# A long convolution by FFT and a gated layer: the exchanged spectrum made by matmuls instead of loaded, and the taps, transposes and first stage in a new order

## The chip, the cores and the metric

The kernel runs on one core of one Trainium2 chip. The metric is device time in microseconds; a lower number is better. A core has a matrix engine (TensorE, PE; its weight loads are listed as PEld), a vector engine (VectorE, DVE), a scalar engine (ScalarE, ACT), GpSimd (POOL) and SyncE (SP), which here only issues DMAs. The engines run side by side, each in its own order of instructions, and wait for each other by semaphores.

## What is computed

All data are float32; the sequence has 2048 rows of 448 channels.

```
mod = (silu(c) @ w_mod)                      # six rows: sa, ca, ga, sb, cb, gb
h   = layernorm(x) * (1 + ca) + sa           # x = A_q
k'  = sum over 4 taps of shift_k[:, t] * k shifted by t rows
kv  = k' * v
y   = irfft(rfft(kv padded to 4096) * rfft(ssm_k padded to 4096))[:2048] + kv * ssm_D
x   = x + ga * h * y
h   = layernorm(x) * (1 + cb) + sb
x   = x + gb * ((sigmoid(h @ w_gate) * (h @ w_up)) @ w_down)
```

## The kernel before

The long convolution is done as a transform in two stages of matmuls. Both the filter (ssm_k, tiles ak[0] and ak[1], one for each half h of the 448 channels) and the product kv (tiles av[0], av[1]) pass through it. Stage 1 (lines 199 and 208) multiplies by a table zc; then `turn` (line 176) transposes 32x32 squares on DVE, 128x896 at a time, eight such pieces to a tile; stage 2 (`stage2`, line 267) multiplies by the table w2, in eight blocks n = 0 to 7 to a half. A block of a spectrum has 128 rows: two groups of 64, and in each 32 rows of real and 32 of imaginary parts.

The order of the work is written out by hand; the scheduler keeps it, and each engine does its part in that order.

**First part, up to about 81 us.** The filter's stage 1 for both halves, DVE's transposes of ak[0], and stage 2 of the filter for half 0 (`stage2_k(0, n)`; matmuls to a PSUM pair "t", copied back by ACT, line 274). ak[1] isn't transposed by DVE: `turn_out` writes it to DRAM (kd) and `turn_in` reads it back in the other order (lines 183, 188). In between stands the short convolution: four groups i of rows by four channel tiles ct of 112 channels. For ct 0 and 1 ACT makes the first tap's product (line 238) and DVE adds the other three (line 240). For ct 2 and 3 ACT makes the products of taps 0 and 3, POOL those of taps 1 and 2 (lines 233, 235), and the four products are added in PSUM by the transposes. `conv_turn` (line 254) transposes the results on PE into the PSUM tiles kv, which take the tags "sa", "y" and "t" in turns; `conv_mul` (line 260) multiplies v by them on DVE. Then stage 1 of v, one matmul pair for each of 16 groups (`stage1_v`), copied out by ACT and, for half 1 from group 8 on, by DVE (line 212).

**Half 0 and half 1 of the product.** `stage2_v(h, between)` makes stage 2 of v for block n and multiplies it by the filter's spectrum. A complex product needs v times the filter (line 303) and v times the filter with real and imaginary rows exchanged (line 304). The exchanged copy kx is loaded by `load_kx`: four DMAs a block from the filter's tile in SBUF to another one, 32 rows each, one block ahead (line 288). `stage2_back` (lines 314 to 316) does the first stage back for the block before it. Between the blocks, `during0` and `during1` put other work: loads of x, `turn_in`, transposes of av, the six rows of mod (`mod_load` DMAs two halves of 392 KB, `mod_parts` and `mod_sum` multiply them on PE and ACT), the statistics of the first layer norm on ACT (`ln1_stats`, two tiles of x at a time, lines 410 and 411), the gate rows G (`gates`: ACT line 430, POOL lines 431 and 432), and for half 1 `stage2_k(1, n)`.

**After that**, `stage_out` (line 325) makes y, gates multiply it into x (lines 338 and 339, on POOL for half 0 and on DVE for half 1), the second layer norm is taken (lines 391 to 404, xn in line 698), and the gated layer runs on PE to the end (lines 739 and 761).

PSUM holds two pairs of banks with the tag "t", one with "sa" and one with "y"; a tile waits until the last reader of the one before it in its tag is done. All loads of this part are issued by SP, in order: a DMA that must wait for its buffer holds up all those behind it.

Of the kernel before, what the change touches and what calls it, by code (L numbers as in the profile page):

```python
# [17 lines left out]
P = 128  # L18
# [6 lines left out]
def _dft_tables():  # L25
# [13 lines left out]
    w2 = np.zeros((128, 64))  # L39
    for r in (0, 64):  # L40
        w2[r:r + 32, :32] = e.real
        w2[r + 32:r + 64, :32] = -e.imag
        w2[r:r + 32, 32:] = e.imag
        w2[r + 32:r + 64, 32:] = e.real
# [36 lines left out]
def adaln_conv_glu_kernel(ctx: ExitStack, tc: tile.TileContext, q, kT, v, ssm, shift, dskip,  # L81
# [66 lines left out]
    w2 = small([P, 64], "w2")  # L148
# [53 lines left out]
    def stage1_v(g):  # L202
# [6 lines left out]
        for h in range(2):  # L209
            a, y = av[h].rearrange("p (s j) c -> p s j c", s=2)[:, :, g], pt[:, :, h * C:h * C + C]  # L210
            if h and g > 7:
                DVE.tensor_copy(a, y)
            else:
                ACT.activation(a, y, AF.Copy)
# [3 lines left out]
    def conv_taps(i, ct, some=(0, 1, 2, 3)):  # L218


        for tap in some:
            x = ktl[:, ct, 4 * i + 3 - tap:4 * i + 7 - tap]
            w = sk[:, ct, tap:tap + 1]
            if tap == 3:
                a = x
            elif tap == 0 or ct > 1:
                a = pk.tile([DT, 4, P], F32, tag="accp" if ct > 1 else "accs", bufs=8 if ct > 1 else 2, name=f"acc{i}_{ct}{tap}")
            else:
                a = acc[i, ct][0]
            if ct > 1:  # L230
                acc.setdefault((i, ct), []).append(a)
                if tap in (0, 3):
                    ACT.activation(a, x, AF.Copy, scale=w)
                else:
                    POOL.tensor_mul(a, x, w.unsqueeze(2).to_broadcast([DT, 4, P]))  # L235
            elif tap == 0:
                acc[i, ct] = [a]
                ACT.activation(a, x, AF.Copy, scale=w)
            else:
                DVE.scalar_tensor_tensor(a, x, w, acc[i, ct][0], op0=OP.mult, op1=OP.add)  # L240
                acc[i, ct] = [a]
# [3 lines left out]
    def conv_turn(i, cts, es=(0, 1)):  # L245

        for e in es:
            if (i, e) not in kvs:
                kvs[i, e] = two((("sa", "y"), ("t", "t"), ("sa", "y"), ("t", "sa"))[i][e], f"kv{i}{e}")
            for ct in cts:  # L250
                parts = acc[i, ct]
                for g in range(2):
                    for k, a in enumerate(parts):
                        PE.matmul(kvs[i, e][:, g, ct * DT:ct * DT + DT], a[:, 2 * e + g], ident[:DT, :DT],
                                  start=k == 0, stop=k == len(parts) - 1, is_transpose=True)
# [6 lines left out]
    def stage2(pt, x):  # L262

        for b in range(2):
            for r in (0, 64):
                c = r ^ 64 * b
                PE.matmul(pt[c:c + 64, b, :D], w2[r:r + 64], x[r:r + 64, b], start=True, stop=True)  # L267

    def stage2_k(h, n):

        x = block(ak[h], n)
        pt = two("t", f"s2k{h}_{n}")
# [8 lines left out]
    kxs = {}  # L281

    def load_kx(h, n):

        kx = quad("kx", 2, f"kx{h}_{n}").rearrange("p a c -> p (a c)").rearrange("p (b j c) -> p b j c", b=2, c=DT)
        x = block(ak[h], n)
        for r in range(0, P, 32):
            nc.sync.dma_start(kx[r:r + 32], x[r ^ 32:(r ^ 32) + 32])  # L288
        kxs[h, n] = kx

    products = []

    def stage2_v(h, between):

        cols4 = lambda t: t.rearrange("p b (j c) -> p b j c", c=DT)
        for n in range(8):
            kx = kxs.pop((h, n))
            if n < 7 or h == 0:
                load_kx(*((h, n + 1) if n < 7 else (1, 0)))
            pt = two("t", f"s2v{h}_{n}")  # L300
            stage2(pt, block(av[h], n))
            m = [pairs(quad("m", 4, f"m{h}_{n}_{k}")) for k in range(2)]
            DVE.tensor_mul(cols4(m[0]), cols4(rows(pt)), block(ak[h], n))  # L303
# [587 lines left out]
```

## Time and profile before

| | |
|---|---|
| runs timed | 657.83 us median of 3 (657.61 to 660.26) |
| profiled execution | 658.9 us, span 657.1 us from first to last instruction |
| mean granted TensorE clock | 0.955 |
| busy, us | PE 583.3, PEld 439.5, DVE 344.0, ACT 254.2, POOL 95.4 |
| DMA | 51.84 MB in 37207 packets, of them 19379 under 512 B |

The page divides the span into slices and gives each engine's busy share; a window of the trace does so for a stretch between two times. The granted clock is the TensorE clock that the throttle let through, 1.00 being full speed. The chain of waits is followed back from the last instruction: each piece is work, a transfer or an issue that what comes next waited for. In a timeline each row has its start in us, its length, the engine, the line of the code, the operation, output and input by name; in brackets stands the idle time before it and what ended that. In a row that ends in "x2" two instructions are merged. f32 matmuls show twice in the records, so eight records of line 267 are the four matmuls of a block.

### The profile page before, as it was taken

To read this page: it belongs to the slowest core of one execution; us is meant where nothing else is said; L and a number is where in the kernel's file an instruction comes from. 1 tells how busy PE (TensorE), PEld (TensorE's weight loads), DVE (VectorE), ACT (ScalarE), POOL (GpSimd) and SP (SyncE) were. 2 spreads that over 40 slices of the span, in tenths; PEclk is the share of its full clock that TensorE was granted. 3 is DMA by queue.
4 is the path that set the end of the run, shared out by engine and by line. 5 is a ranking of instruction groups with operands and counts; after the bars stand their busy time and mean duration, and the time that the engine had idled before them with its cause. 6 is when DMAs were issued, how large, how long until landed. Compare 5 with 4: busy or idle time off the path is not lost.

```text
span 657.1 us, 7479 instructions
## 1 busy us (share of the span) xinstructions
PE 583.3 (89%) x2976; PEld 439.5 (67%) x2976; DVE 344.0 (52%) x403; ACT 254.2 (39%) x448; POOL 95.4 (15%) x65
## 2 busy tenths in 40 slices
PE   7867875489854998999999999999999999999995
PEld 6445311123333776888888888888888888888884
DVE  0998496488988875543234443244333433333322
ACT  4874466258742657851122222122112212221110
POOL 1282002200998100000000000010001000000000
PEclk9998977699987997999999999999999999999999
DMA  8994599958610110000001111011101100000122
GB/s 294 237 297 136 167 265 256 219 115 197 170 57 16 60 33 1 0 1 0 1 29 48 31 30 49 0 29 33 32 15 30 33 17 18 11 0 1 57 83 84
DMA packets 37207, 51.84 MB, mean 79 GB/s; under 512 B 19379, under 2 KB 25909, under 8 KB 37045
## 3 DMA queue, kind: packets, MB, share of 16 engines
q1 hardware_dynamic: 37108, 51.36, 29.2%
q8 instruction: 23, 0.38, 0.2%
q14 instruction: 12, 0.09, 0.0%
q0 software_dynamic: 64, 0.01, 0.0%
HBM read 36.68 MB, written 7.34 MB: 67 GB/s over the span
## 4 chain that ended last, share of the span: by engine, by line
PE 62%; DVE 10%; ACT 8%; DMA 5%; issue 2%; SPq 1%; DVEq 0%; ACTq 0%
PE gu L739 37%; PE d L761 19%; DVE av L176 3%; DMA kx<-ak 3%; DMA wb<-in_wmod_dram 2%; PE sa L314 1%; SPq L288 1%; PE s2v L267 1%; DVE xn L698 1%; PE y L325 1%; DVE x L339 1%; PE s2k L267 1%; ACT xn L700 1%; ACT full L720 1%; DVE wt L469 1%
## 5 line engine op out<-in xcount | busy, mean ns | idle before, releaser
L739 PE MATMUL gu<-xt,wt 128*128 128x512 f32 x1232 | 292.4, 391 | 0.6 <-DVE xt L728 0.6
L739 PEld LDWEIGHTS gu<-xt,wt 128*128 128x128 f32 x1232 | 231.0, 188 | 48.6 <-DVE xt L728 1.1
L743 DVE TENSOR_TENSOR sg<-sg,gu 128x512 f32<-128x512 f32 x56 | 38.5, 688 | 190.4 <-ACT sg L742 190.3
L761 PE MATMUL d<-wt,hh 128*128 128x448 f32 x448 | 129.6, 371 | 6.5 <-ACT wt L463 3.2
L742 ACT ACTIVATE sg<-gu 128x512 f32<-128x512 f32 x56 | 33.5, 598 | 240.6 <-PE gu L739 240.5
L761 PEld LDWEIGHTS d<-wt,hh 128*128 128x128 f32 x448 | 84.9, 190 | 17.6 <-ACT wt L463 3.7
L761 PE MATMUL d<-wt,hl 128*128 128x448 f32 x224 | 82.8, 369 | 0.1
L762 DVE TENSOR_TENSOR x<-x,d 128x896 f32<-128x896 f32 x56 | 60.5, 1080 | 6.4 <-PE d L761 6.4
L747 DVE TENSOR_TENSOR hl<-sg,hh 128x512 fp32r<-128x512 f32 x56 | 38.8, 693 | 39.2 <-ACT hh L746 39.2
L462 POOL TENSOR_TENSOR r<-r,gbrow 128x448 f32<-128x448 f32 x10 | 11.5, 1158 | 319.4 <-DMA r<-in_wd_dram 319.4
L176 DVE STREAM_TRANSPOSE av<-av 128x896 f32<-128x896 f32 x32 | 56.9, 1835 | 0.0
L746 ACT ACTIVATE hh<-sg 128x512 fp32r<-128x512 f32 x56 | 35.4, 633 | 47.2 <-DVE sg L743 47.2
L761 PEld LDWEIGHTS d<-wt,hl 128*128 128x128 f32 x224 | 42.7, 190 | 3.8 <-DVE hl L747 0.4
L315 PE MATMUL sa<-m,wa 128*64 128x448 f32 x64 | 31.9, 627 | 5.5 <-DVE m L304 5.5
L314 PE MATMUL sa<-m,wa 128*64 128x448 f32 x64 | 31.4, 613 | 3.6 <-DVE m L303 2.3
L431 POOL TENSOR_TENSOR G<-G,arow 128x896 f32<-128x896 f32 x8 | 18.5, 2308 | 99.5 <-ACT G L430 51.0
L267 PE MATMUL s2k<-ak,w 64*64 64x448 f32 x128 | 17.1, 579 | 13.5 <-DMA kx<-ak 7.8
L235 POOL TENSOR_TENSOR acc<-kT,sk 112x512 f32<-112x512 f32 x16 | 22.1, 1409 | 18.1 <-DMA kT<-in_kT_dram 13.3
L325 PE MATMUL y<-av,wb 128*64 128x224 f32 x128 | 15.4, 398 | 9.7 <-DVE av L176 9.0
L304 DVE TENSOR_TENSOR m<-s2v,kx 128x896 f32<-128x896 f32 x16 | 17.4, 1089 | 12.4 <-DMA kx<-ak 12.4
L314 PEld LDWEIGHTS sa<-m,wa 128*64 128x64 f32 x64 | 7.9, 149 | 23.5 <-issue 12.9
L316 ACT ACTIVATE av<-sa 128x896 f32<-128x896 f32 x16 | 14.6, 911 | 22.5 <-PE sa L315 22.5
(108 smaller groups left out, 568.5 us busy)
## 6 DMA issues: line engine op xcount, KB each, us to landing
kx<-ak SPq DMA_DIRECT2D x64, 112.0 KB, 5.2
kd<-ak SPq DMA_DIRECT2D x4, 896.0 KB, 7.1
x<-in_q_dram SPq DMA_DIRECT2D x4, 896.0 KB, 10.1
ak<-kd SPq DMA_DIRECT2D x4, 896.0 KB, 12.7
out_dram<-x SPq DMA_DIRECT2D x8, 448.0 KB, 2.5
wb<-in_wmod_dram SPq DMA_DIRECT2D x8, 392.0 KB, 7.0
v<-in_v_dram SPq DMA_DIRECT2D x6, 448.0 KB, 12.4
r<-in_wg_dram SPq DMA_DIRECT2D x10, 256.0 KB, 2.7
```

The source lines that it names most:

```text
L176: DVE.transpose(x, x)
L235: POOL.tensor_mul(a, x, w.unsqueeze(2).to_broadcast([DT, 4, P]))
L267: PE.matmul(pt[c:c + 64, b, :D], w2[r:r + 64], x[r:r + 64, b], start=True, stop=True)
L314: PE.matmul(pt[0:64, b, :D], wa[:, b, 0:64], m1[:, b], start=True, stop=True)
L315: PE.matmul(pt[64:128, b, :D], wa[:, b, 64:128], m2[:, b], start=True, stop=True)
L739: PE.matmul(pgu[:, s], w[:, t, f * P:(f + 1) * P], x[:, xs], start=i == 0, stop=i == len(ops) - 1)
L742: ACT.activation(sg, pgu[:, 0], AF.Sigmoid)
L743: DVE.tensor_mul(sg, sg, pgu[:, 1])
L746: ACT.activation(hh, sg, AF.Copy)
L747: DVE.tensor_sub(hl, sg, hh)
L761: PE.matmul(pt[:, i, :D], h[:, (2 * e + i) * P:(2 * e + i + 1) * P], w[:, f], start=m == 0, stop=m == len(ops) - 1)
L762: DVE.tensor_add(x1[:, g:g + 2], x1[:, g:g + 2], rows(pt))
```

## The change

Three things are changed, and the order around them.

1. The table w2 becomes two: the second has the columns of real and imaginary output exchanged. `stage2_v` multiplies every block of v by both and so gets v and its exchanged form, in two PSUM pairs "t" (one for each group of 64 rows' parity b). DVE multiplies each pair by the filter's block, which is repeated over the two forms by a stride of zero. `load_kx` and its 64 DMAs are gone. `stage2_k` for half 1 uses the tag "y" instead of "t".
2. POOL makes no tap products. For ct 2, group 0 uses matmuls by a diagonal matrix of the taps (made once by POOL, in arow), groups 1 to 3 have four ACT products added by the transposes; ct 3 has that in group 0 and ACT and DVE like ct 0 and 1 in the others. So ACT makes 27 products instead of 24 and DVE 33 adds instead of 24.
3. Stage 1 of v starts between the groups of the short convolution, the tiles kv always take "sa" and "y", and ACT copies groups 8 and 9 of half 1, which DVE did. The turn-in of ak[1] and the loads of x move ahead of the halves; the rows of mod, the statistics and the gate rows come at other blocks, and row 4 already in block 1.

```diff
-    w2 = np.zeros((128, 64))
+    w2 = np.zeros((128, 2, 64))
     for r in (0, 64):
...
+        x = np.block([[e.real, e.imag], [-e.imag, e.real]])
+        w2[r:r + 64, 0] = x
+        w2[r:r + 64, 1] = np.roll(x, 32, 1)
...
-            if h and g > 7:
+            if h and g > 9:
                 DVE.tensor_copy(a, y)
...
+    def conv_first(i, ct):
+        acc[i, ct] = [pk.tile([DT, 4, P], F32, tag="accs", bufs=3, name=f"acc{i}_{ct}")]
+        ACT.activation(acc[i, ct][0], ktl[:, ct, 4 * i + 3:4 * i + 7], AF.Copy, scale=sk[:, ct, 0:1])
+    def conv_rest(i, ct):
+        for tap in range(1, 4):
             x = ktl[:, ct, 4 * i + 3 - tap:4 * i + 7 - tap]
+            a = x if tap == 3 else acc[i, ct][0]
+            DVE.scalar_tensor_tensor(a, x, sk[:, ct, tap:tap + 1], acc[i, ct][0], op0=OP.mult, op1=OP.add)
+        acc[i, ct] = [a]
+    def conv_products(i, ct):
+        acc[i, ct] = []
+        for tap in range(4):
+            x = ktl[:, ct, 4 * i + 3 - tap:4 * i + 7 - tap]
+            a = x if tap == 3 else pk.tile([DT, 4, P], F32, tag="accp", bufs=6, name=f"acp{i}_{tap}")
+            ACT.activation(a, x, AF.Copy, scale=sk[:, ct, tap:tap + 1])
+            acc[i, ct].append(a)
...
-                kvs[i, e] = two((("sa", "y"), ("t", "t"), ("sa", "y"), ("t", "sa"))[i][e], f"kv{i}{e}")
+                kvs[i, e] = two(("sa", "y")[e], f"kv{i}{e}")
...
+                    if (i, ct) not in acc:
+                        for tap in range(4):
+                            PE.matmul(y, ktl[:, ct, 4 * i + 3 - tap + 2 * e + g], diag[:, tap], start=tap == 0, stop=tap == 3)
...
     def stage2_k(h, n):
-        pt = two("t", f"s2k{h}_{n}")
+        pt = two("y" if h else "t", f"s2k{h}_{n}")
...
         for n in range(8):
-            kx = kxs.pop((h, n))
-            if n < 7 or h == 0:
-                load_kx(*((h, n + 1) if n < 7 else (1, 0)))
-            pt = two("t", f"s2v{h}_{n}")
-            stage2(pt, block(av[h], n))
-            m = [pairs(quad("m", 4, f"m{h}_{n}_{k}")) for k in range(2)]
-            DVE.tensor_mul(cols4(m[0]), cols4(rows(pt)), block(ak[h], n))
-            DVE.tensor_mul(cols4(m[1]), cols4(rows(pt)), kx)
+            x, k = block(av[h], n), block(ak[h], n)
+            pts = [two("t", f"s2v{h}_{n}_{b}") for b in range(2)]
+            for ex in range(2):
+                for b in range(2):
+                    for r in (0, 64):
+                        c = r ^ 64 * b
+                        PE.matmul(pts[b][c:c + 64, ex, :D], w2[r:r + 64, ex], x[r:r + 64, b], start=True, stop=True)
+            m = [pairs(quad("m", 4, f"m{h}_{n}_{b}")) for b in range(2)]
+            for b in range(2):
+                DVE.tensor_mul(cols4(m[b]), cols4(rows(pts[b])), k[:, b].unsqueeze(1).to_broadcast([P, 2, 4, DT]))
...
     def during0(n):
...
-        if n < 4:
-            turn_in(ak[1], kd, (n,))
...
+        if n > 1:
+            stage2_k(1, n - 2)
+        if n < 2:
+            mod_parts({0: 2, 1: 4}[n], "y")
+            mod_load({0: 3, 1: 5}[n])
+        if n in (1, 2, 6):
+            ln1_end({1: 0, 2: 1, 6: 2}[n])
+        if n in (2, 4, 6):
             next(gating)
+        if n not in (2, 4, 6):
+            ln1_stats({0: 2, 1: 3, 3: 4, 5: 5, 7: 6}[n])
...
-        if 2 <= n < 8:
+        if 1 <= n < 6:
             next(gating)
```

What stands in the engines' orders now: first the loads on SP, from the last turn-out of ak[1] to the loads for block 2 of half 0. wb and wm are halves of the rows of mod (wb also holds two tiles of v), x_670 and x_629 are x. Before:

```order
L183 DMA kd<-ak_150 256x1x896 x2
L351 DMA wb<-in_wmod_dram 112x896 x2
L351 DMA wm_671<-in_wmod_dram 112x896
L351 DMA wm_673<-in_wmod_dram 112x896
L585 DMA x_670<-in_q_dram 128x1792
L595 DMA wa<-in_wat_dram 128x256
L288 DMA kx_0_705<-ak_149 32x8x112 x4
L351 DMA wm_710<-in_wmod_dram 112x896
L351 DMA wm_712<-in_wmod_dram 112x896
L288 DMA kx_1_754<-ak_149 32x8x112 x4
L585 DMA x_670<-in_q_dram 128x1792
L188 DMA ak_150<-kd 32x32x224
```

In the changed kernel, behind the same turn-out and up to row 4 of mod (wm_700, with its second half behind it):

```order
L187 DMA ak_154<-kd 32x32x224 x2
L344 DMA wm_621<-in_wmod_dram 112x896
L344 DMA wm_623<-in_wmod_dram 112x896
L581 DMA x_629<-in_q_dram 128x1792
L590 DMA wa<-in_wat_dram 128x256
L344 DMA wb<-in_wmod_dram 112x896 x2
L344 DMA wm_662<-in_wmod_dram 112x896
L344 DMA wm_664<-in_wmod_dram 112x896
L581 DMA x_629<-in_q_dram 128x1792
L187 DMA ak_154<-kd 32x32x224 x2
L581 DMA x_629<-in_q_dram 128x1792 x2
L344 DMA wm_700<-in_wmod_dram 112x896
```

The read-back of ak[1] and all of x now stand ahead of row 4, and the exchanged copies are gone.

Then PE around block 2 of half 0; s2v is the second stage of v, sa the first stage back, s2k the filter's second stage for half 1, and mod_903 and mod_775 are row 4. Before:

```order
L371 MATMUL mod_772<-part_781,ones 128x448
L267 MATMUL s2v_2_823<-av_484,w_78 64x448 x4
L314 MATMUL sa_1_832<-m_1_0_795,wa 64x448
L315 MATMUL sa_1_832<-m_1_1_796,wa 64x448
L314 MATMUL sa_1_832<-m_1_0_795,wa 64x448
L315 MATMUL sa_1_832<-m_1_1_796,wa 64x448
L267 MATMUL s2v_3_859<-av_484,w_78 64x448 x4
```

In the changed kernel:

```order
L364 MATMUL mod_731<-part_740,ones 128x448
L355 MATMUL mod_775<-wm_700,scb 32x224 x4
L355 MATMUL mod_775<-wm_702,scb 32x224 x4
L293 MATMUL s2v_2_0_795<-av_405,w_78 64x448 x2
L293 MATMUL s2v_2_1_796<-av_405,w_78 64x448 x2
L293 MATMUL s2v_2_0_795<-av_405,w_78 64x448 x2
L293 MATMUL s2v_2_1_796<-av_405,w_78 64x448 x2
L308 MATMUL sa_1_809<-m_1_0_760,wa 64x448 x2
L308 MATMUL sa_1_809<-m_1_1_761,wa 64x448 x2
L374 MATMUL mod_775<-ones,part_784 128x1 x3
L376 MATMUL mod_775<-ones,part_784 64x1 x2
L266 MATMUL s2k_0_823<-ak_154,w_78 64x448 x4
```

Row 4's matmuls now stand ahead of block 2's second stage, where they stood behind block 4; s2v has twice the matmuls, and s2k of the other half follows from block 2 on, not from block 4.

More of the change, by code (lines that the diff above doesn't have):

```diff
@@ L488, in adaln_conv_glu_kernel @@
     POOL.tensor_mul(sc, sc, cv)
+    diag = arow[:DT].rearrange("p (a d) -> p a d", d=DT)
+    for tap in range(4):
+        POOL.tensor_mul(diag[:, tap], ident[:DT, :DT], sk[:, 2, tap:tap + 1].to_broadcast([DT, DT]))
     POOL.tensor_copy(scb, sc.unsqueeze(2).to_broadcast([DT, 4, 32]))
@@ L512, in adaln_conv_glu_kernel @@
         load_v(k)
[L513 to L518 removed]
     kd = pd.tile([P, 32, C], F32, name="kd")
+    for i in range(2):
+        turn_out(ak[1], kd, i)
     av = []
```

209 lines of the change are left out of this document (80 added, 129 removed).

## Prediction

> **What bounds the kernel now.** I read the busy shares over the span first, then the windows of four stages, then the chain of waits, the DMA view, and the timelines of DVE and PE. The change touches nothing behind the run-up to the last stage, so what can move lies in the first 212 us. The stages by window (columns: length, then busy us of PE, PEld, DVE, ACT and POOL, then granted clock, DMA share, GB/s), the two halves of the spectrum product first, then the run-up to the last stage, then the taps and first stage of v:
>
> ```profile
> 88.20:145.50 57.30, 39.38 (x206) 11.10 (x208) 38.46 (x34) 29.96 (x65) 8.34 (x4) 0.76 0.97 211
> 145.50:181.40 35.90, 31.72 (x236) 11.21 (x237) 32.53 (x30) 28.51 (x56) 17.51 (x9) 1.00 0.73 181
> 181.40:211.90 30.50, 14.22 (x104) 9.07 (x100) 28.07 (x27) 11.48 (x21) 29.69 (x14) 0.78 0.10 32
> 24.10:81.20 57.10, 43.80 (x304) 25.11 (x304) 46.54 (x44) 34.84 (x58) 22.10 (x16) 0.94 0.71 205
> ```
>
> Half 0 takes 57 us, half 1 36 us for the same eight blocks. In half 0 no engine is busy over 40 of the 57 us, but the DMA engines are (0.97). The chain of waits says the same:
>
> ```profile
> 91.33 12.24 DMA wb<-in_wmod_dram
> ...
> 105.52 9.12 DMA kx<-ak
> ...
> 122.75 6.04 DMA kx<-ak
> ```
>
> One queue carries all of it. Its loads (count, KB each, us to landing), and its rate from 92 to 128 us:
>
> ```profile
> kx<-ak SPq DMA_DIRECT2D x64, 112.0 KB, 5.2
> kd<-ak SPq DMA_DIRECT2D x4, 896.0 KB, 7.1
> x<-in_q_dram SPq DMA_DIRECT2D x4, 896.0 KB, 10.1
> ak<-kd SPq DMA_DIRECT2D x4, 896.0 KB, 12.7
> wb<-in_wmod_dram SPq DMA_DIRECT2D x8, 392.0 KB, 7.0
> ```
> ```profile
> DMA packets 8937, 8.64 MB, mean 240 GB/s; under 512 B 4279, under 2 KB 8375, under 8 KB 8936
> ```
>
> The landmarks for the sum are on DVE: the last copy of the first stage, the five transposes, the first product of half 0, of half 1, and the last product:
>
> ```profile
> 80.69 0.62 DVE L212 COPY av<-s1v 128x448 f32<-128x448 f32 x1 [0.60 <-ACT av L214]
> 81.23 8.60 DVE L176 STREAM_TRANSPOSE av<-av 128x896 f32<-128x896 f32 x5
> 89.72 1.06 DVE L303 TENSOR_TENSOR m<-s2v,ak 128x896 f32<-128x896 f32 x1
> ...
> 145.56 1.09 DVE L303 TENSOR_TENSOR m<-s2v,ak 128x896 f32<-128x896 f32 x1 [0.86 <-issue]
> ...
> 180.33 1.08 DVE L304 TENSOR_TENSOR m<-s2v,kx 128x896 f32<-128x896 f32 x1
> ```
>
> So before: first stage to 81.3, 8.4 to the first product, half 0 55.9, half 1 35.8 (to 181.4), run-up 30.4 (to 211.8, below), and 445.3 of what I leave alone.
>
> **The taps and the first stage.** One tap add on DVE beside a GpSimd product, and two stretches after GpSimd had stopped:
>
> ```profile
> 42.70 2.97 DVE L240 SCALAR_TENSOR_TENSOR acc<-kT,sk,acc 112x512 f32<-112x512 f32 x2
> ...
> 60.27 0.75 DVE L240 SCALAR_TENSOR_TENSOR kT<-kT,sk,acc 112x512 f32<-112x512 f32 x1
> 60.94 2.08 DVE L260 TENSOR_TENSOR wb<-wb,kv 128x896 f32<-128x896 f32 x2
> 62.93 1.53 DVE L240 SCALAR_TENSOR_TENSOR acc<-kT,sk,acc 112x512 f32<-112x512 f32 x2
> ```
>
> An add costs 1.48 beside GpSimd and 0.77 without it. The change drops the 16 GpSimd products (22.1 us, row of 24.10 above) and makes 33 adds where there were 24. DVE is free of its first transposes at 30.5 as before; from there 33 x 0.77 = 25.4, 8 products x 1.04 = 8.3, and six copies where there were eight, at the pace of 1.17 of the copies before 81.3, 7.0: 71.2. ACT in turn gets 27 tap products for 24 and two more copies (line, engine, shapes, count, busy, mean ns; those of L430, L411 and L410 are used further down):
>
> ```profile
> L430 ACT ACTIVATE G<-x,nmr,rstd 128x224 f32<-128x224 f32 x32 | 15.7, 564 | 1.0 <-DVE nmr L419 1.0
> ...
> L274 ACT ACTIVATE ak<-s2k 128x896 f32<-128x896 f32 x16 | 14.4, 908 | 9.4 <-PE s2k L267 9.4
> ...
> L214 ACT ACTIVATE av<-s1v 128x448 f32<-128x448 f32 x24 | 12.0, 548 | 11.5 <-PE s1v L208 11.5
> ...
> L411 ACT ACTIVATE gbrow<-x,nmr 128x448 f32<-128x448 f32 x16 | 10.7, 670 | 0.5
> ...
> L410 ACT ACTIVATE gbrow<-x 128x448 f32<-128x448 f32 x16 | 9.2, 575 | 0.3
> ...
> L238 ACT ACTIVATE acc<-kT,sk 112x512 f32<-112x512 f32 x8 | 5.8, 721 | 0.7 <-DVE kT L240 0.7
> ```
>
> 27 x 0.72 + 8 x 0.91 + 26 x 0.55 = 41 us from 25 on: 66, less than DVE. The tap results now always go to the same two PSUM pairs, so the transposes of group i+1 wait for the products of group i; I add 1.8 for these hand-overs. The 16 matmuls with the diagonal are not in the trace; the nearest are the transposes they replace in part, which PE has room for until DVE frees the second half of the spectrum at 30.5: nothing. The first stage ends at 73.0, 8.3 earlier; bounds 71.2 and, if the hand-overs eat it all, 81.3 (not later, since both engines have less work in sum than the 57 us there).
>
> **First product.** Five transposes, 8.6, end at 81.6. PE reaches it through two modulation rows, the first of which now stands behind x, wa and another row in the queue; I take 1 us for that and put the first product at 82.5, 9.5 behind the copies (+1.1).
>
> **Half 0.** The 64 kx loads (7.3 MB) go, and with them the waits of the chain. In their place PE makes the exchanged spectrum. One block of PE before:
>
> ```profile
> 135.31 0.98 PE L267 MATMUL s2k<-ak,w 64*64 64x448 f32 x8
> 136.12 0.93 PE L267 MATMUL s2v<-av,w 64*64 64x448 f32 x8
> 136.98 0.59 PE L314 MATMUL sa<-m,wa 128*64 128x448 f32 x1
> ...
> 138.63 0.98 PE L267 MATMUL s2k<-ak,w 64*64 64x448 f32 x8
> ```
>
> From start to start: s2k 0.81, s2v 0.86, sa 1.65. The new s2v is twice that, 1.72, so a block is 4.2 with s2k and 3.4 without. The two products of a block keep size and count; a factor repeated by a zero stride is new, and I price it by the rows of 1.06 and 1.08. Both PSUM pairs "t" now serve one block, so s2v of block n+1 waits for the products of block n; sa, s2k on PE and the transposes on DVE lie in that gap.
>
> Blocks 0 and 1 are DVE's: 2.0 for the products and 3.5 for two transposes each, 82.5 to 93.5, and two row products, 1.3: 94.8. Then PE has modulation row 4 ahead of s2v of block 2, and that row now stands in the queue behind everything: from the last turn-out on, four ak<-kd, four x, eight halves of modulation rows, 10.7 MB with wa. The turn-out waits only for the first four groups of the first stage: 30.5, nine adds and two products (9.0), and for each group ACT's two copies and its share of the tap products, about 2, in all about 48; v and kd are then issued (1.4) and kd lands 7.1 later (its row): 56.5. At 250 GB/s, a little over the 240 of the row since no 448-byte packets are among them, 42.8 us: row 4 lands at 99.3, not by 94.8. Bounds for the landing: 96 (three quarters of the bytes at 300 or more) and 102 (240, one us late). This rate is where the Trainium skill speaks differently. "DMA: Bandwidth & Descriptors", Specifications, gives about 358 GB/s from HBM for a core and line rate from 512 bytes a packet, which these packets of 896 bytes and more all pass; by an estimate from it the 10.7 MB would take 30 us and row 4 would be there by 87, a rival below.
>
> So row 4 (1.0) and most of s2v (1.5) follow 99.3, and block 2's products start at 101.8. Block 3 stands behind ACT, since its s2k waits in the single "y" pair for the row's results: part 0.5, statistics of two tiles 2 x (0.58 + 0.67 + two accumulator reads) = 3.1, the copy of sa 0.9, columns, copy of s2k: 5.8, 107.6. From there each block costs ACT two copies of 0.9 and either statistics (3.1, three blocks) or a gate row (4 x 0.49, two blocks): 4.4; PE 4.2, DVE 2.0 + 1.75. Five blocks at 4.4: 129.6. Half 0 is 47.1 instead of 55.9: -8.8.
>
> **Half 1.** kx no longer limits it, but it was DVE's before (32.5 of 35.9 us) and stays so. Block to block: 4.1 (PE), 5.8, then 5.5 three times (products and two transposes), 3.4 behind s2v (y, 1.7 on PE, in between), 4.9, and 2.0: 36.7, +0.9.
>
> **Run-up.** Lines of DVE before, and what GpSimd was doing:
>
> ```profile
> 181.33 12.12 DVE L176 STREAM_TRANSPOSE av<-av 128x896 f32<-128x896 f32 x7
> ...
> 198.08 2.18 DVE L339 TENSOR_TENSOR x<-x,G 128x896 f32<-128x896 f32 x1
> ...
> 203.23 1.15 DVE L404 SCALAR_TENSOR_TENSOR nmr<-mv,rstd 128x4 f32<-128x4 f32 x1
> 204.31 0.68 DVE L469 TENSOR_TENSOR wt<-tmp,wt 128x512 fp32r<-128x512 f32 x1
> 204.91 6.90 DVE L698 TENSOR_SCALAR xn<-x,rstd,nmr 128x448 f32<-128x448 f32 x4
> ...
> 219.54 1.09 DVE L339 TENSOR_TENSOR x<-x,G 128x896 f32<-128x896 f32 x1
> ```
> ```profile
> 209.05 2.51 POOL L462 TENSOR_TENSOR tmp<-tmp,gbrow 128x448 f32<-128x448 f32 x2
> ```
>
> The same x<-x,G is 2.18 while GpSimd works and 1.09 after it. In the change the statistics come earlier, and with them GpSimd's 24 gate operations of 2.1 (8.34 for four, row of 88.20). The last gate row is ready about 158, ten such operations and the 2.5 above follow: 182. xn would start 23.5 behind the last product as before (204.9 - 181.4), less what x and nmr save, at 188: GpSimd is done some 5 us ahead of it. Then x saves 1.1, nmr 1.0, and xn falls from 6.9 to between 6.9 (no gain) and four of the 0.62 of the copy of equal size, 2.5; I take 2.5 as the nearest: -6.5 in all. "VectorE: DVE Perf Modes", in its perf-mode tier table of the Trainium skill, has such an operation at 1227 ns for 2048 columns, by an estimate 0.3 for 448; by it xn would be 1.1, 1.4 us better still. The other DVE lines and the last stage stay.
>
> **Sum.** -8.3 + 1.1 - 8.8 + 0.9 - 6.5 = -21.6. The profiled execution took 658.9 (span 657.1), 1.1 over the median of the three runs: 658.9 - 21.6 - 1.1 = 636.
>
> **Rivals.**
> Row 4 lands in time: then block 2 starts 4.5 earlier, at the row products' end, and the time is 632; with the other upper ends (first stage at 71.2) 627. For it: half of the packets behind the 240 were the 448-byte ones that go. Against: 211 and 205 over whole stretches, the second with none of them. The skill's figure above would give this case.
>
> The first stage stays as long: hand-overs through one pair of PSUM tiles and an in-order SP queue, where x and all behind it wait for the last tap tile. Then the queue, too, starts 8 us later: 636 + 8.3 = 644, and 651 if GpSimd's end also falls behind xn (6.5). For it: ACT and DVE alternate with PE after every group. Against: DVE was busy 46.5 of 57 us there, 11 of them lost to GpSimd and more in waits.
>
> Slower than before: PE becomes the bound at a low clock. Per block PE, DVE and PE again alternate through the same two pairs; PE has 16 x 3.4 + 8 x 0.8 + about 9 for modulation and y = 70 us at full clock in both halves. The gains outside them are 13.7, so the halves may take 91.7 + 13.7 = 105: below a mean granted clock of 0.67 the kernel is slower; at 0.60 it would be 117 and 669 in all. The row of half 0 shows 0.76 with long DMA waits, that of half 1 1.00 with PE at 88%. With fuller PE I expect the latter. "TensorE: Matmul & The Clock Gate", the part on psum-queue depth-cycling, describes this throttling from short idles between groups; by half 1's row it does not happen here.
>
> **How the numbers follow.** Forecast (630 to 643) 0.47, row 4 in time (624 to 632) 0.25, first stage without gain (643 to 651) 0.18, below 624 0.02, no change 0.05 (nearly every gain lost; within 0.5%, about what a measurement of this kernel can tell), slower 0.03. The range reaches over the first three: 624 to 649. Faster by over 0.5% is 0.92, same 0.05, slower 0.03.
>
> **What would show it.** Right: tap adds at 0.75 throughout; last copy of the first stage at 71 to 75; the wait of the chain near 95 to 100 on modulation row 4, none on kx; blocks 3 to 7 at 4.2 to 4.6; half 1 near 37; xn well under 1 us each, GpSimd done before them. Wrong: a granted clock under 0.7 in the halves, the first product after 88, half 0 over 52, GpSimd still busy beside xn.

## The result, and the profile after

The changed kernel takes 639.18 us (median of 4 runs, 637.25 to 640.29), the kernel before 657.95 beside it: a ratio of 0.9704, 95% interval 0.9672 to 0.9737. Predicted were 636.0 and 624 to 649. The profiled execution took 639.4 (span 637.6, before 657.1).

The stretches by window of the trace (length, busy us of PE, PEld, DVE, ACT and POOL with their instructions, then granted clock, DMA share, GB/s): taps and first stage, the way to the first product, half 0, half 1, run-up.

```profile
24.10:70.00 45.90, 39.48 (x268) 21.64 (x260) 41.65 (x52) 36.39 (x62) 0.00 (x0) 0.96 1.00 291
70.00:86.50 16.50, 10.52 (x56) 2.88 (x60) 8.39 (x5) 6.59 (x17) 0.00 (x0) 0.59 1.07 264
86.50:129.40 42.90, 36.92 (x278) 13.38 (x280) 37.43 (x36) 32.45 (x70) 10.38 (x5) 0.92 0.38 106
129.40:167.60 38.20, 36.16 (x276) 14.10 (x278) 32.32 (x28) 26.19 (x53) 26.75 (x14) 1.00 0.21 75
167.60:192.20 24.60, 14.20 (x103) 9.27 (x99) 23.92 (x26) 9.92 (x17) 16.22 (x9) 0.79 0.12 33
```

The transfers that filled half 0 (share 0.97) now fill the two stretches ahead of it. Half 0 is bound by the engines, and the new weak place is the row of 70.00, where every engine waits and TensorE has a granted clock of 0.59. The landmarks on DVE, the same as those of before: last copy of the first stage, first product, blocks 1 to 3, first product of half 1, last product, and the run-up:

```profile
68.61 1.38 DVE L211 COPY av<-s1v 128x448 f32<-128x448 f32 x2 [0.95 <-ACT av L213]
...
86.53 2.09 DVE L296 TENSOR_TENSOR m<-s2v,ak 128x896 f32<-128x896 f32 x2 [8.14 <-PE s2v L293]
...
91.91 2.10 DVE L296 TENSOR_TENSOR m<-s2v,ak 128x896 f32<-128x896 f32 x2
...
97.66 0.68 DVE L367 TENSOR_TENSOR brow<-brow,mod 128x448 f32<-128x448 f32 x1
...
103.39 2.09 DVE L296 TENSOR_TENSOR m<-s2v,ak 128x896 f32<-128x896 f32 x2 [4.77 <-PE s2v L293]
...
109.12 2.08 DVE L296 TENSOR_TENSOR m<-s2v,ak 128x896 f32<-128x896 f32 x2
...
129.39 2.09 DVE L296 TENSOR_TENSOR m<-s2v,ak 128x896 f32<-128x896 f32 x2 [0.16 <-PE s2v L293]
...
165.53 2.09 DVE L296 TENSOR_TENSOR m<-s2v,ak 128x896 f32<-128x896 f32 x2 [1.15 <-PE s2v L293]
...
179.46 5.14 DVE L462 TENSOR_TENSOR wt<-tmp,wt 128x512 fp32r<-128x512 f32 x3
184.52 1.07 DVE L331 TENSOR_TENSOR G<-G,y 128x896 f32<-128x896 f32 x1
185.63 1.09 DVE L332 TENSOR_TENSOR x<-x,G 128x896 f32<-128x896 f32 x1
...
190.39 1.78 DVE L684 TENSOR_SCALAR xn<-x,rstd,nmr 128x448 f32<-128x448 f32 x4
```

| stretch, us | before | predicted | after |
|---|---|---|---|
| end of the first stage | 81.3 | 73.0 | 70.0 |
| from there to the first product | 8.4 | 9.5 | 16.5 |
| half 0 | 55.9 | 47.1 | 42.9 |
| half 1 | 35.8 | 36.7 | 38.2 |
| run-up, to the end of xn | 30.4 | 23.9 | 24.6 |
| the rest | 445.3 | 445.3 | 445.4 |

The gains stand where they were expected, but three terms missed, by -3.0, 7.0 and -4.2 us, and cancel: that the sum came within 3.2 us of the time is in part luck. The column "before" is one execution. In three experiments below that keep the old taps and run-up (the spectrum alone and the two that follow it) the first stage ended at 76.2 to 78.5 and the run-up took 28.4 to 29.1, so these two gains lie between 6 and 11 us and between 4 and 6. The two waits that are left show on PE:

```profile
74.23 0.97 PE L355 MATMUL mod<-wb,scb 112*32 112x224 f32 x8 [5.49 <-DMA wb<-in_wmod_dram]
75.51 0.97 PE L355 MATMUL mod<-wb,scb 112*32 112x224 f32 x8 [0.31 <-DMA wb<-in_wmod_dram]
77.20 1.86 PE L364 MATMUL mod<-part,ones 128*128 128x448 f32 x2 [0.71 <-ACT part L357]
78.99 1.72 PE L355 MATMUL mod<-wm,scb 112*32 112x224 f32 x16
81.44 1.86 PE L364 MATMUL mod<-part,ones 128*128 128x448 f32 x2 [0.72 <-ACT part L357]
83.23 3.27 PE L293 MATMUL s2v<-av,w 64*64 64x448 f32 x16
...
98.44 1.72 PE L355 MATMUL mod<-wm,scb 112*32 112x224 f32 x16 [5.45 <-DVE rstd L411]
100.09 3.27 PE L293 MATMUL s2v<-av,w 64*64 64x448 f32 x16
```

The first is plain: row 1 of mod lands at 74.2, and its matmuls, its sum, row 0's and its sum all stand ahead of the first s2v. The second needs care. Row 4's matmuls (98.44) need two things: row 4 itself, and the PSUM pair "y", which DVE reads last in L367 (97.66 + 0.68 = 98.34, above). DVE's order puts that behind two transposes. When row 4 was issued, and how long it took to land (two halves):

```profile
L344 SPq DMA_DIRECT2D wm<-in_wmod_dram x2: 338/392/445, 82.0 to 83.0; - x2
...
DMA to landing us min/median/max: 15.3/15.6/15.8
```

So the first half landed at 97.3 to 97.8 and the second, which is needed about 0.9 later, at some 98.6. Load and PSUM pair came free within a microsecond of each other; by these times, removing only one would have gained under 1 us. The bracket names L411, another instruction of DVE right behind L367.

### The profile page after: what moved, and what is told of

It reads as the page before. It is cut to its first block, busy times and chain, and to the rows that moved or that the text cites. A ratio compares the mean times of both kernels' runs of the same rounds, so it can differ in the third digit from the quotient of the medians.

```text
span 637.6 us, 7551 instructions
## 1 busy us (share of the span) xinstructions
PE 589.6 (92%) x3084; PEld 443.8 (70%) x3084; DVE 335.7 (53%) x410; ACT 256.1 (40%) x453; POOL 72.1 (11%) x53
## 4 chain that ended last, share of the span: by engine, by line
PE 59%; DVE 7%; ACT 6%; issue 1%; DVEq 0%; ACTq 0%
PE gu L725 39%; PE d L747 20%; DVE wt L462 2%; ACT xn L686 1%; ACT full L706 1%; DVE sg L729 1%; DVE x L332 1%; DVE x L748 1%; DVE G L331 1%; ACT xt L710 1%; ACT hh L732 1%; ACT sq L385 1%; PE pt L698 1%; DVE xt L712 1%; DVE av L175 1%
## 5 line engine op out<-in xcount | busy, mean ns | idle before, releaser
L296 DVE TENSOR_TENSOR m<-s2v,ak 128x896 f32<-128x896 f32 x32 | 33.2, 1079 | 18.2 <-PE s2v L293 18.0
L293 PE MATMUL s2v<-av,w 64*64 64x448 f32 x256 | 33.6, 596 | 1.8 <-DVE m L296 1.6
L424 POOL TENSOR_TENSOR G<-G,arow 128x896 f32<-128x896 f32 x8 | 16.9, 2108 | 115.4 <-ACT G L423 115.4
L308 PE MATMUL sa<-m,wa 128*64 128x448 f32 x128 | 27.7, 554 | 0.0
L293 PEld LDWEIGHTS s2v<-av,w 64*64 64x64 f32 x256 | 11.8, 143 | 19.1 <-issue 10.9
L308 PEld LDWEIGHTS sa<-m,wa 128*64 128x64 f32 x128 | 7.9, 138 | 18.9 <-issue 9.6
L318 PEld LDWEIGHTS y<-av,wb 128*64 128x64 f32 x128 | 11.3, 161 | 13.8 <-issue 10.5
L462 DVE TENSOR_TENSOR wt<-r,wt 128x512 fp32r<-128x512 f32 (+1 forms) x30 | 19.7, 661 | 0.0
```

The costliest lines, as they stand in the source:

```text
L293: PE.matmul(pts[b][c:c + 64, ex, :D], w2[r:r + 64, ex], x[r:r + 64, b], start=True, stop=True)
L296: DVE.tensor_mul(cols4(m[b]), cols4(rows(pts[b])), k[:, b].unsqueeze(1).to_broadcast([P, 2, 4, DT]))
L308: PE.matmul(pt[r, b, :D], wa[:, b, r], m[b][:, ex], start=True, stop=True)
L462: DVE.tensor_sub(lo, r, hi)
```

## The experiments

The theory is the prediction's: three gains that add up (the taps without GpSimd, half 0 without kx and with its loads ahead, a run-up that GpSimd no longer slows), and two waits. The rivals: one part alone does it; the queue bounds half 0 in any order; TensorE's doubled work is what limits now. In each run the kernel before was timed on the same chip, and the ratios are to it. Two experiments may stand on different chips, where the kernel before took 657.7 to 659.4, so differences between their medians are good to some 1.7 us.

### The exchanged spectrum alone

The kernel before, with the doubled w2, `stage2_v` and the tag of s2k as in the change; row 4's matmuls and the sums of rows 3, 4 and 5 of mod are shifted by a block so that "y" is free for s2k.

```diff
-            kx = kxs.pop((h, n))
...
+            for ex in range(2):
+                for b in range(2):
+                    for r in (0, 64):
+                        c = r ^ 64 * b
+                        PE.matmul(pts[b][c:c + 64, ex, :D], w2[r:r + 64, ex], x[r:r + 64, b], start=True, stop=True)
...
-        pt = two("t", f"s2k{h}_{n}")
+        pt = two("y" if h else "t", f"s2k{h}_{n}")
```

> The kernel before with only the exchanged spectrum made on PE (no kx loads; the products of rows 3, 4 and 5 of mod a step earlier or later, so that the pair y is free); taps, first stage and order as before. Theory (the kx loads were what half 0 waited for): half 0 falls from 55.9 to about 46, half 1 gains 1 to 2, first stage and run-up stay: about 649. Rival 1 (the new order is what pays, and the loads would have been hidden): 655 to 661. Rival 2 (all of the gain is this part): 637 to 641.

656.53 us, ratio 0.9958 (0.9927 to 0.9988): the theory's 649 is missed, and the time is that of the first rival. From its DVE:

```profile
122.97 2.09 DVE L296 TENSOR_TENSOR m<-s2v,ak 128x896 f32<-128x896 f32 x2 [10.25 <-PE s2v L293]
...
142.54 2.09 DVE L296 TENSOR_TENSOR m<-s2v,ak 128x896 f32<-128x896 f32 x2 [4.14 <-issue]
```

and from PE, what held block 5:

```profile
118.22 1.02 PE L266 MATMUL s2k<-ak,w 64*64 64x448 f32 x3 [5.61 <-DMA ak<-kd]
```

Half 0 took 49.1 us (87.18 to 136.31) instead of 55.9, half 1 43.7 instead of 35.8. The loads of kx were gone, but the read-back of ak[1], issued one piece a block, now came last; and half 1 gave back 7.9 us.

### Read-back and x ahead of half 0, in the old order

The kernel above, with these loads moved.

```diff
     mod_load(2)
+    load_x(1)
+    turn_in(ak[1], kd, range(4))
+    for i in range(2, 4):
+        load_x(i)
...
-            load_x(n + 1)
-        if n < 4:
-            turn_in(ak[1], kd, (n,))
```

> The kernel before with the exchanged spectrum on TensorE (656.5 us), and beside that only the read-back of ak[1] and the loads of x issued ahead of half 0 in one piece, as the changed kernel does, instead of one in each of its first blocks. Theory (of the gain in half 0 that the spectrum on TensorE should have given, most was lost because block 5 waited 10 us behind the read-back, which SyncE issued late): half 0 falls from 55.4 to 44 to 48 us, and the time is 646 to 650 us. Rival (half 0 needs the changed kernel's order of the statistics, gates and GpSimd's products too): 652 to 657 us.

654.89 us, 0.9967 (0.9932 to 1.0003): no measurable difference from the one above; the theory's 646 to 650 is missed. (The 55.4 there is counted one block too long; by the landmarks used elsewhere it is 49.1.) Half 0 took 48.6 (54.8 by that count, outside the 44 to 48), half 1 42.3. PE:

```profile
113.11 1.85 PE L355 MATMUL mod<-wb,scb 112*32 112x224 f32 x16 [7.46 <-DMA wb<-in_wmod_dram]
...
159.94 0.98 PE L266 MATMUL s2k<-ak,w 64*64 64x448 f32 x8 [2.66 <-ACT gbrow L369]
```

The read-back is in time, and row 4, now issued behind it, is last: one wait has taken the place of the other. The second line is one of the waits of half 1: s2k, a row's sum and the next row's matmuls go one after another through the single pair "y", each with ACT in between. Before, s2k used "t".

### And row 4 at the end of half 0

```diff
-        if n == 3:
-            mod_parts(4, "y")
-            mod_load(3)
-        if n == 4:
+        if n == 7:
             mod_sum(4)
...
+        if n == 6:
+            mod_parts(4, "y")
+            mod_load(3)
```

> The last kernel again (the kernel before, the spectrum on TensorE, read-back and x issued ahead of half 0: 654.9 us), with row 4 of mod used at the end of half 0 instead of in block 3. In its trace, block 4 waited 8.2 us, since row 4, which SyncE now issues behind the read-back and x at 98.5 us, landed at 113. Theory (half 0 lost the gain of the spectrum on TensorE to whatever the queue brings last ahead of block 4: the read-back first, row 4 next; with all of it in time, the blocks run at their pace of 4 to 5.5 us): half 0 falls from 54.8 to 45 to 48 us, and the time is 646 to 649 us. Rival (ScalarE's statistics or GpSimd's work hold half 0 in the old order, and no transfer): 652 us or more.

653.7 us, 0.9926 (0.9895 to 0.9956): the rival's number, and in part its place. (Again a block too long: the 54.8 is 48.6.) Half 0 is 45.8, which by the count of the expectation is 52.0 and outside its 45 to 48; half 1 is 43.8. Blocks 3 to 5 now follow each other at 4.0, but one long wait remains in half 0, on DVE and with its cause in ACT's statistics, as the rival had it:

```profile
126.07 2.09 DVE L296 TENSOR_TENSOR m<-s2v,ak 128x896 f32<-128x896 f32 x2 [6.87 <-PE s2v L293]
```
```profile
117.85 0.57 ACT L403 ACTIVATE gbrow<-x 128x448 f32<-128x448 f32 x1
...
121.04 0.90 ACT L273 ACTIVATE ak<-s2k 128x896 f32<-128x896 f32 x1
```

Row 4's matmuls wait for "y", which ACT frees only behind its statistics (117.85 to 121.0). So the spectrum on TensorE is worth 7 us in half 0 alone and 10 with these loads out of the way, and in the old order nearly all of it goes again in half 1, where four s2k still stand, through the pair "y". The changed kernel has two of them there, and 38.2 us. That the pair is what costs half 1 those us is read from the waits; it was not tried alone.

### GpSimd's tap products put back

The changed kernel, with taps 1 and 2 of the eight products on GpSimd.

```diff
+            if tap in (1, 2):
+                POOL.tensor_mul(a, x, sk[:, ct, tap:tap + 1].unsqueeze(2).to_broadcast([DT, 4, P]))
+            else:
                 ACT.activation(a, x, AF.Copy, scale=sk[:, ct, tap:tap + 1])
```

> The changed kernel with taps 1 and 2 of the four product sets (8 products) on GpSimd again instead of ACT. Theory (a GpSimd product costs DVE's adds beside it some 0.7 each): 5 to 6 us more in the first stage, of which the wait for row 1 of mod ahead of the first product (DVE idle 8.1) covers a part: 640 to 643, adds at 1.4 where GpSimd works. Rival (the order, not GpSimd, shortened the first stage): within 1 of the changed kernel's 639.2, adds at 0.77.

642.67 us, 0.9761 (0.9728 to 0.9794), within the theory's range: +3.5 for eight products. DVE, an add beside a product, one without, and the last copy:

```profile
36.91 1.41 DVE L227 SCALAR_TENSOR_TENSOR kT<-kT,sk,acc 112x512 f32<-112x512 f32 x1
...
39.81 0.75 DVE L227 SCALAR_TENSOR_TENSOR kT<-kT,sk,acc 112x512 f32<-112x512 f32 x1
...
73.11 1.38 DVE L211 COPY av<-s1v 128x448 f32<-128x448 f32 x2 [0.95 <-ACT av L213]
```

The adds beside GpSimd take 5.1 us more in sum, and the last copy ends 4.5 later (74.5), a little under the 5 to 6 expected. The first product (90.2) follows by 3.6; half 0 takes 45.0 instead of 42.9, so that the halves end 5.8 later.

### Row 4 behind block 3

```diff
-        if n in (1, 2):
-            mod_sum({1: 2, 2: 4}[n])
+        if n in (1, 4):
+            mod_sum({1: 2, 4: 4}[n])
...
-            mod_parts({0: 2, 1: 4}[n], "y")
+        if n in (0, 3):
+            mod_parts({0: 2, 3: 4}[n], "y")
```

> The changed kernel with the matmuls of row 4 of mod two blocks later (block 3 instead of 1, its sum in block 4); loads in the same order. Theory (the queue's last load, row 4, holds up block 2): the wait of 4.8 before block 2 goes, half 0 from 42.9 to 38 or 39: about 635. Rival (ACT's or PE's pace takes the wait back, or the next load in the queue takes its place): within 1 of 639.2.

635.43 us, 0.9644 (0.9609 to 0.9679): -3.7 in the medians, though the intervals touch, and -4.5 of span. The wait ahead of block 2 is gone and half 0 is 39.9 us:

```profile
98.06 2.08 DVE L296 TENSOR_TENSOR m<-s2v,ak 128x896 f32<-128x896 f32 x2
...
125.78 2.09 DVE L296 TENSOR_TENSOR m<-s2v,ak 128x896 f32<-128x896 f32 x2 [0.16 <-PE s2v L293]
```

It moves the row away from both things it waited for, and so does not tell them apart.

### Without the exchanged form's matmuls

This leaves out half of the new work on TensorE: both products take the straight form.

```diff
-            for ex in range(2):
+            for ex in range(1):
```

> The changed kernel without the matmuls for the exchanged form: half of the second stage's matmuls on v are left out and both products use the plain form, so the output is not the reference's. PE has 16 x 0.86 = 13.8 us less. Theory (PE sets the pace of blocks 3 to 7 and of five blocks of half 1, DVE the others): 4 to 7 us less, 632 to 635. Rival 1 (PE is hidden behind DVE and ACT): under 2 less. Rival 2 (PE is the bound of both halves): 12 or more less.

635.84 us, 0.966 (0.9616 to 0.9703): 3.3 by the medians, between theory and first rival, though the intervals overlap. In the trace row 1 landed 2.8 us later than in the changed kernel and the first product came 1.4 later; half 0 was 42.7 us (42.9), half 1 37.8 (38.2). So what TensorE's doubled work costs in the halves lies between 0.6 us (the trace) and some 3 (the medians): small against the 13.8 us of work left out, and far from a bound.

### Rows 1, 0 and 2 inside half 0, and the weight subtractions behind xn

```diff
-    mod_parts(1, "y")
-    mod_sum(1)
-    mod_parts(0, "sa")
-    mod_sum(0)
...
+        if n in (1, 2, 3):
+            mod_sum({1: 1, 2: 0, 3: 2}[n])
+        if n < 3:
+            mod_parts({0: 1, 1: 0, 2: 2}[n], "y")
```

> The changed kernel, with rows 1 and 0 of mod taken out of the stretch between the last transpose and the first product of half 0 and put behind its blocks 0 and 1; row 2 behind block 2, row 4 in half 1. Theory (the first product waits for nothing but the chain row 1's load, its matmuls, its sum, row 0's matmuls, its sum, all ahead of it on TensorE): the transposes end at 78.3 us as before, the first product comes at 80 to 82 instead of 86.5, the wait for row 4 ahead of block 2 is gone too, and half 0 with the additional row takes 39 to 42 us: 629 to 632 us against the changed kernel's 639.2. Rival (transfers bound half 0 whatever stands ahead of it: the read-back of ak[1], x and the rows bring the stretch to its end at the same time): the 5 us come back as waits inside half 0, and the time is 634 us or more, as with row 4 alone moved (635.4).

637.19 us, 0.9681 (0.9608 to 0.9755): not the theory's 629 to 632, but the number of the rival. The first product came at 80.6, as the theory said, but half 0 grew to 44.5 and half 1, which got row 4, to 41.2. A second kernel has the rows inside too, and in the run-up the subtractions behind xn:

```diff
-    for k in range(3):
-        split_lo(0, k)
     gate(1, 0, y1[0], DVE)
...
     norm_rows(0)
+    for k in range(4):
+        split_lo(0, k)
```

> The kernel with the rows inside, and with the three weight subtractions of the run-up (5.14 us in the changed kernel, 1.9 of work) put behind the four xn. Theory (they are slow because GpSimd's last multiplications run beside them, and the gate's two operations, 1.1 us each, would run beside GpSimd in their place at 2.1 each): the run-up loses 2 to 3.5 us, so 627 to 629 us if the rows inside give 630 to 632. Rival (something else ends the run-up: the copies on ScalarE, or the output stage on TensorE behind the last transpose): less than 1 us.

635.14 us, 0.9661 (0.9601 to 0.972). The run-up fell from 24.3 to 22.6, by a little less than the 2 to 3.5 us expected, since DVE now waits in their place:

```profile
180.54 1.09 DVE L331 TENSOR_TENSOR G<-G,y 128x896 f32<-128x896 f32 x1 [3.40 <-POOL tmp L455]
```

The bracket names GpSimd, whose last operation ended at 180.48. PE, whose output y the line reads, had done the first quarter of it (16 of 64 records) at 180.45 by the trace, at a granted clock of 0.50 to 0.60 behind 8 us of idleness. Which of the two was last stays open.

### GpSimd kept busy beside the run-up

The changed kernel; behind GpSimd's last work, with no reader:

```diff
+        for i in range(9):
+            POOL.tensor_mul(brow, brow, arow)
```

> The changed kernel, with nine multiplications of one 128x448 row on GpSimd behind its last piece of work, so that it stays busy for some 9 us more, beside the run-up; nothing reads what they make. Theory (the run-up became shorter because GpSimd is done before xn, so that VectorE's operations aren't slowed): x, nmr and xn go back to what they took before (2.2, 1.15 and 1.7 us each instead of 1.1, 0.17 and 0.44), the run-up is 5 to 8 us longer, and the time is 644 to 647 us. Rival (the run-up became shorter by the new order alone): under 641 us.

642.8 us, 0.9791 (0.9711 to 0.9871). DVE and GpSimd:

```profile
185.24 1.09 DVE L332 TENSOR_TENSOR x<-x,G 128x896 f32<-128x896 f32 x1
...
190.30 5.02 DVE L684 TENSOR_SCALAR xn<-x,rstd,nmr 128x448 f32<-128x448 f32 x4
```
```profile
183.62 12.69 POOL L794 TENSOR_TENSOR brow<-brow,arow 128x448 f32<-128x448 f32 x9
```

The time is between theory and rival. xn takes 1.26 each instead of 0.44, but x is not slowed: +3.5 in the run-up, under the 5 to 8 expected. With GpSimd operations of the size that stood there before:

```diff
+    for i in range(5):
+        POOL.tensor_mul(gt[0, 3], gt[0, 3], arow[:, :C].unsqueeze(1).to_broadcast([P, 4, C]))
```

> The changed kernel with five more multiplications of 128x896 on GpSimd behind its last gate (2.1 us each, the size that the kernel before had beside xn); they overwrite a tile whose values are no longer read. With operations of 128x448 (1.13 us each) beside them, the four xn took 5.0 us in all instead of 1.8, x and nmr the same as without. Theory (VectorE's operation waits for the end of the GpSimd operation that runs, so a GpSimd operation of twice the size costs more): the four xn take 6 to 7.5 us, x about 2.2, nmr about 1, so the run-up is 6 to 7.5 us longer: 645 to 647 us. Rival (the price does not depend on the size): about 642.5 us, as with the short ones.

645.62 us, 0.9808 (0.9757 to 0.9858), within the theory's range.

```profile
179.26 6.98 DVE L462 TENSOR_TENSOR wt<-tmp,wt 128x512 fp32r<-128x512 f32 x3
...
187.28 1.89 DVE L332 TENSOR_TENSOR x<-x,G 128x896 f32<-128x896 f32 x1
...
192.14 1.12 DVE L397 SCALAR_TENSOR_TENSOR nmr<-mv,rstd 128x4 f32<-128x4 f32 x1
193.19 0.68 DVE L462 TENSOR_TENSOR wt<-tmp,wt 128x512 fp32r<-128x512 f32 x1
193.79 3.39 DVE L686 TENSOR_SCALAR xn<-x,rstd,nmr 128x448 f32<-128x448 f32 x4
```

Not by the items expected, though: the long operations were over at 193.25, ahead of xn, and slowed L462, x and nmr instead; xn had only the short ones beside it (3.39 for four). The run-up is 5.2 us longer than the changed kernel's, not 6 to 7.5. Which of two operations is slowed goes by which one runs first. Here x started at 187.28 inside a GpSimd operation and ended 0.95 behind its end; with the short operations x started at 185.24, just ahead of one, and it was that one which took 2.04 instead of 1.13. The two GpSimd operations, this kernel's first:

```profile
185.78 2.44 POOL L666 TENSOR_TENSOR G<-G,arow 128x896 f32<-128x896 f32 x1
...
185.29 2.04 POOL L794 TENSOR_TENSOR brow<-brow,arow 128x448 f32<-128x448 f32 x1
```

### Only row 1 inside

```diff
-    mod_parts(1, "y")
-    mod_sum(1)
     mod_parts(0, "sa")
...
+        if n in (1, 2, 4):
+            mod_sum({1: 1, 2: 2, 4: 4}[n])
...
+        if n in (0, 1, 3):
+            mod_parts({0: 1, 1: 2, 3: 4}[n], "y")
```

The weight subtractions stand behind xn here too.

> The changed kernel (639.2 us) with only row 1 of mod moved behind block 0 of half 0 (row 0 stays ahead of the first product, on a TensorE that waits for transposes there), row 2 behind block 1, row 4 behind block 3, and the three weight subtractions of the run-up behind xn. With rows 1, 0 and 2 all inside, and row 4 in half 1, the first product came at 80.6 instead of 86.5, but half 0 grew to 44.5 and half 1 to 41.2 us, from 42.9 and 38.2. Theory (those 5 us were the price of where the rows were put: matmuls that waited for VectorE's product with row 2 in the bank they share, and statistics shifted in half 1; not transfers): first product at 80 to 82, half 0 of 40 to 42 us, half 1 of 38 to 39 us, and 1.5 to 2 us less in the run-up, together 628 to 631 us. Rival (half 0 is bound by what the queue brings, whatever the order): half 0 of 44 us or more, and 633 us or more.

635.07 us, 0.9654 (0.9601 to 0.9708): the first product at 81.0, half 1 38.4 and the run-up 22.7, as expected, but half 0 45.9, so that half 0 and the time are the rival's. PE ahead of block 3, and DVE:

```profile
99.00 1.89 PE L266 MATMUL s2k<-ak,w 64*64 64x448 f32 x8 [4.01 <-DVE rstd L411]
```
```profile
98.22 0.63 DVE L367 TENSOR_TENSOR brow<-brow,mod 128x448 f32<-128x448 f32 x1
```

Here s2k starts right behind brow (98.85): the pair "y" again, or the read-back that s2k needs, whose last part was issued at 76.3 and took 18.9 us, so it landed at 95.2.

### The sum ahead of the transposes

```diff
     def during0(n):
+        if n in (1, 2, 4):
+            mod_sum({1: 1, 2: 2, 4: 4}[n])
         if n < 3:
             turn(av[0], 5 + n)
         turn(av[1], n)
-        if n in (1, 2, 4):
-            mod_sum({1: 1, 2: 2, 4: 4}[n])
```

> The last kernel (row 1 inside, weight subtractions behind xn: 635.1 us), with the sum of a row placed ahead of the two transposes of its block instead of behind them, so that VectorE multiplies arow and brow before it transposes. There TensorE stood 4.0 us ahead of block 3, from 94.99 to 99.00, right behind the end of brow on VectorE at 98.85: the spectrum's matmuls need the PSUM bank that VectorE still reads, and block 3's matmuls stand behind them. Theory (the bank, freed by VectorE in its order, and not the queue): brow ends at 96.0 to 96.5, the wait falls from 4.0 to 1 to 1.5 us, half 0 from 45.9 to 42 to 43.5 us, and the time is 632 to 633.5 us. Rival (the read-back of ak[1], which those matmuls read, lands only then: its last part was issued at some 76 to 77 us and took 18.9): the wait stays above 3 us and the time at 634.5 or more.

630.34 us, 0.9587 (0.9543 to 0.9632), below the theory's range; 8.8 less than the changed kernel, and the fastest here. DVE and PE:

```profile
80.14 2.09 DVE L296 TENSOR_TENSOR m<-s2v,ak 128x896 f32<-128x896 f32 x2 [1.71 <-PE s2v L293]
...
93.81 0.61 DVE L367 TENSOR_TENSOR brow<-brow,mod 128x448 f32<-128x448 f32 x1
...
122.68 2.09 DVE L296 TENSOR_TENSOR m<-s2v,ak 128x896 f32<-128x896 f32 x2
```
```profile
94.57 1.89 PE L266 MATMUL s2k<-ak,w 64*64 64x448 f32 x8 [2.10 <-DVE brow L367]
```

s2k follows brow again by under 0.2 us, now 4.4 us earlier on the clock; the wait is 2.1 instead of 4.0, half 0 42.5 instead of 45.9. In this execution the queue ran earlier too:

```profile
L187 SPq DMA_DIRECT2D ak<-kd x4: 322/454/4850, 56.2 to 72.1; - x4
...
DMA to landing us min/median/max: 6.4/10.4/19.1
```

The last part of the read-back, issued at 72.1, landed at 91.2, so the earlier start alone would not tell the two apart. But in both kernels the read-back was there over 3 us ahead of s2k, and brow ended under 0.2 us ahead of it. So it was DVE's order and the pair "y", not the read-back. Against the changed kernel: -6.4 at the first product, -0.4 in half 0, 0.1 in half 1, -1.9 in the run-up, together -8.6 of the 9.0 of span.

## Why the prediction was right, and where its steps were off

**Taps and first stage: right, mis-sized.** The adds are 0.75 throughout, and the eight products put back show the price of GpSimd beside them. Of the 1.8 us for hand-overs 1.2 came (0.69 and 0.51, each a wait for kv ahead of a product); DVE began 0.5 earlier than taken, and the last six copies, in three pairs of 1.3 to 1.4, 2.3 from pair to pair, took 6.0 for 7.0: 70.0 for 73.0.

**First product: the step that failed.** "I take 1 us for that" stands for row 1, which moved behind a read-back, x, wa and row 0 in the queue. It landed at 74.2; two rows and their sums followed on a TensorE with a granted clock of 0.59, to 83.2. The cost was 8.1 instead of 1.1. With only row 1 behind block 0 the first product comes at 80 to 81.

**Half 0: the direction right, the size and one cause off.** Row 4 was forecast to land at 99.3; its halves landed near 97.6 and 98.6. "DMA: Bandwidth & Descriptors" of the Trainium skill, Specifications (about 358 GB/s), would have had it there by 87, by the estimate in the prediction; the trace disagrees, with 256 GB/s over 54 to 100 us at a DMA share of 1.02. What the step missed is the PSUM pair "y", which DVE held to 98.34. It changed the number little here, but became the whole wait once row 4 was out of the way. Blocks 4 to 7 ran at 4.07, not at 4.4: ACT's work fitted beside PE's. And as the first product came 4.0 later than forecast (86.5 for 82.5), and the queue did not, less of the wait was left for half 0: one miss paid for a part of the other.

**Half 1: 38.2 for 36.7.** The wait was ahead of block 2: 1.1 for ACT's statistics on DVE, then two transposes, so 7.0 us for that block instead of 5.8.

**Run-up: right, with two sizes off.** GpSimd's end was forecast for 182 and came at 184.0, still 6 us ahead of xn. xn is 0.44 each, between the 0.62 taken and the 0.3 estimated by the perf-mode tier table of "VectorE: DVE Perf Modes" of the Trainium skill. But GpSimd's last work now falls beside the three subtractions of L462: 5.14 instead of 1.88. Keeping GpSimd busy costs 3.5 to 5.2 us of the 4 to 6 gained, so this gain is the absence of GpSimd and not of the order alone.

**The rivals.** The first stage without gain, and a TensorE at low clock, did not come: the clock was 0.92 and 1.00 in the halves. Row 4 in time did not come either, and alone it would have gained under 1 us, since "y" was held as long; its matmuls moved away from both waits gained 3.7 us (4.5 of span), about what that rival gave. (Its lower figure of 627 does not follow from the term that it names: a first stage at 71.2 saves 1.8, so 630.)

**The parts do not add.** The spectrum on TensorE alone gained 1 to 5 us of the 19; the rest of what it makes possible needs the earlier queue and s2k out of half 1.

## What to carry to other kernels

When a load that holds up a stage is removed, look for the transfer and the PSUM tile that are next in line: here kx gave way to the read-back, that to row 4, and that to a pair of banks that an in-order engine freed late. A small piece of work (two rows, 4 us of matmuls) ahead of a stage costs its load's landing and its chain through two engines; put it behind the first block, and let the engine that frees a PSUM tile do so before its long work. A bracket names only what the profile saw last: compare the end of each thing that the waiting instruction needs.

## What the runs showed of the hardware

- The read-back's 896-byte packets come at little over half the rate of the x right behind them: 225 GB/s over 79 to 90 us of the changed kernel, 395 over 89.8 to 93. The rows behind x came at 273 (96 to 100), so the size of the packets is not all. The rates over 54 to 100 us, in 40 slices: by SP's order the stretches near 210 are the two parts of the read-back, and the 382 to 418 ahead of the end are x.

```profile
GB/s 27 71 277 213 203 209 208 200 214 221 252 287 284 386 328 266 274 284 293 321 293 382 224 213 206 208 210 206 220 223 240 382 418 405 256 228 262 281 262 290
```

- A wait on TensorE costs a second time: behind 5 us of idleness the sixteen records of s2v took 3.27 us instead of 1.68, and behind 8 us the output stage ran at a granted clock of 0.50 to 0.60. "TensorE: Matmul & The Clock Gate" of the Trainium skill, Part 1, has half the clock from an idle window of about 3.4 us on; the trace agrees.
- Beside GpSimd, DVE's xn (1.26 for 0.44) and the tap adds (1.41 for 0.75) are slowed, and G<-G,y of L331, which reads PSUM, in no run (1.07 to 1.09). In these traces the one of x<-x,G and GpSimd's operation that starts second pays: x<-x,G took 1.89 when it started inside a GpSimd operation, and 1.09 when it started 0.05 us ahead of one, which then took 2.04 for 1.13.
